# Another order of loads and side steps in an attention and two-MoE kernel: k and v over all partitions, rests of their own, a first h product in parts

## The chip, the cores and the metric

One core of one Trainium2 chip runs the kernel. The metric is device time of one execution in microseconds (us), lower is better. The engines are TensorE (PE, matmuls and transposes; PEld is its weight load), VectorE (DVE), ScalarE (ACT), GpSimd (POOL) and SyncE (SP, which here only issues DMAs). Each works through its own queue in order.

## What is computed

The reference in short:

```python
# q, k, v: [4, 8, 576, 64]
kv  = einsum('bhsd,bhse->bhde', k, v)
o   = einsum('bhsd,bhde->bhse', q, kv)
o   = o / sqrt(mean(o * o, -1) + 1e-6) * g_norm
x   = o.transpose(0, 2, 1, 3).reshape(2304, 512)
h   = x @ w_in                                  # [2304, 1024]
e   = exp(h - max(h));  so = h * e / (sum(e) + 1e-9)
ln  = (so - mean(so)) / sqrt(var(so) + 1e-6) * g_ln
x2  = ln @ w_out                                # [2304, 512]
out = ((x2 @ w_a) * (x2 @ w_b)) @ w_out2        # inner width 1536
```

The weights come as float64 and are made float32 on the chip.

## The kernel before

**Tiles.** The 2304 tokens are 18 tiles of 128. A batch has 576 tokens: four tiles of 128 and a rest of 64; the rests of two batches share a tile.

**Precision.** Most products are three matmuls: an operand is split into a high part (a copy by ACT into a shorter format, `split`, `x_hi`, `l_hi`) and a low part (source minus high, by DVE or POOL, lines 50, 423, 508, 552), and high x high, high x low, low x high are summed in PSUM.

**Weights.** `fetch` (line 272) loads a 128 x 512 block of float64 into one of five places of `ring`; a place is free again when the block that it held is narrowed. `begin` takes the absolute value on ACT (line 62), the class `Narrow` then clamps (line 67, DVE, or POOL where the order says BP), shifts (82), sets the sign (88) and adds the low bits (93) on DVE; `mid` does these steps for one block (M) or two side by side (MM), and `end` splits the block, its low part on POOL (E) or DVE (EV).

**Attention and first MoE.** These run by an order written out by hand, in the strings `PROLOGUE` (tiles 0 to 4), `SLOT` and `LATER` (one pass a tile). A token is a step: LK, LQ, LW load k and v, q, a weight block; kp multiplies a pair of heads of k and v and kk (DVE) or ka (ACT) keeps it; qt, qk turn q; op, os, om, ox are the o product, its squares, the root of the mean square (small steps on DVE, then ten on POOL) and the scaling (DVE); xt, xh, xl turn x and split it; hp is the h product (24 matmuls), hm, he, hs, hq, hn its maximum, exponential, product with it, squares and norm; lt0, lt1, lh0, ... turn and split the norm; yp, yk are the output product and its copy. "+2" is the tile two further on. An order string fixes the order on each engine's queue; between engines semaphores do.

**Loads of k and v.** `load_kv` loads half of the heads of a batch. The 576 rows of a head are laid over the partitions so that partitions 0 to 63 hold five rows and 64 to 127 hold four; so a tensor takes two DMAs, one for each half of the partitions (lines 317 and 318), and the fifth place of the upper half is zero, filled once (line 308). `kv_product` then does five chunks of two heads (line 342). Every third LK token does nothing.

**Second MoE.** It takes 6 tiles at once (s = 0, 1, 2) and two blocks of the inner width (j = 0 to 5). `quad(j, s, m, side)` is one product with w_a (m = 0) or w_b (m = 1), done as seven smaller products of six matmuls each, with additions by DVE between them (lines 740 to 765); the seventh is left open and closed in the quad that follows, after its third product. After each of the first six products `tick` runs some steps of the list `side` (weight narrowing, sums, splits for later quads), evenly dealt, and those that `then` put into `delayed` under t1 to t6, the tick's number. The last round prepares the output product, which `out_pair` does at the end (line 881).

Of the kernel before, what the change touches and what calls it, by code (L numbers as in the profile page):

```python
# [30 lines left out]
hp+2 qk+5 om+4 hq+1 E lh0 LW E xh+3 B MM lt1 LK ox+4 hn+1 hm+2 qt+6 ll0 he+2 lh1 qt+7 kp B xl+3 op+5  # L31
hs+2 kp hp+3 os+5 hq+2 om+5 ll1 hn+2 xt+4 LQ E qk+6 MM LK ka qk+7 B E kp lt0+1 lt1+1 ka xh+4 hm+3
ox+5 he+3 xl+4 op+6 lh1+1 ka lt1+2 lh0+1 B hs+3 ll0+1 os+6 lh1+2 E MM E ll1+1 lt0+2 xt+5 om+6 B EV
EV hp+4 BP hq+3 lh0+2 hm+4 he+4 ox+6 hn+3 hs+4 ll1+2 xh+5 yp yp yp yp xl+5 ll0+2 lt0+3 lt1+3 hq+4
lh0+3 yk yk hn+4 LK M yk E M ll0+3 B lh1+3 ll1+3 BP yk
"""
# [16 lines left out]
class Narrow:  # L53
# [47 lines left out]
def tile_attention_moe(ctx, tc, q, k, v, g_norm, w_in, w_out, g_ln, w_a, w_b, w_out2, out):  # L101
# [201 lines left out]
    KJ = -(-S // P)
    LONG = S - (KJ - 1) * P
    kv_tiles = [[ld.tile([P, H // 2, KJ, D], F32, name=f"{nm}s{n}", bufs=1) for nm in "kv"] for n in range(2)]
    for ts in kv_tiles:
        for t in ts:
            nc.gpsimd.memset(t[LONG:, :, KJ - 1, :], 0.0)
# [37 lines left out]

    def kv_keep(copy=nc.vector.tensor_copy):
# [42 lines left out]

    def o_rms(i):
# [4 lines left out]
        rms[i] = rsqrt(ms, H, "a")  # L396

# [33 lines left out]

    def h_product(i):
        xh, xl = xT.pop(i)
        ph = ps_h.tile([P, 2, HALF], F32, tag="h", name="ph")
        order = [(n, c) for n in range(2) for c in range(NK)]
        for n, c in order if i == 0 else sorted(order, key=lambda nc_: nc_[1]):
# [4 lines left out]
        hs_[i] = dict(ph=ph.rearrange("p a b -> p (a b)"))  # L441

# [546 lines left out]
    def load_gl(_):  # L989
# [178 lines left out]
    def half(n, part, eng=nc.vector):  # L1168
        return hi_lo(wo2, n, eng, part)
# [18 lines left out]
    for n, k in ((XB11, 0), (XT1, 1)):  # L1188
# [112 lines left out]
```

## Time and profile before

| | |
|---|---|
| time, median of 3 runs | 700.51 us (699.49 to 701.65) |
| profiled execution | 702.19 us, span 700.1 us |
| PE | 665.7 us busy, 95% of the span, 4710 instructions |
| PEld | 633.0 us, 90% |
| DVE | 519.6 us, 74% |
| ACT | 284.1 us, 41% |
| POOL | 302.8 us, 43% |
| mean granted PE clock | 0.995 of full speed |
| DMA | 103.84 MB, mean 148 GB/s |

The span is from the first to the last instruction of the profiled execution; the time has some 2 us more around it. Busy shares are means over stages with different limits: the start (loads and narrowing of w_in), the attention with the first MoE, the second MoE's rounds, and the output product. So the rows are read by stage.

### The profile page before, as it was taken

To read this page: it belongs to the slowest core of one execution; us is meant where nothing else is said; L and a number is where in the kernel's file an instruction comes from. 1 tells how busy PE (TensorE), PEld (TensorE's weight loads), DVE (VectorE), ACT (ScalarE), POOL (GpSimd) and SP (SyncE) were. 2 spreads that over 40 slices of the span, in tenths; PEclk is the share of its full clock that TensorE was granted. 3 is DMA by queue.
4 is the path that set the end of the run, shared out by engine and by line. 5 is a ranking of instruction groups with operands and counts; after the bars stand their busy time and mean duration, and the time that the engine had idled before them with its cause. 6 is when DMAs were issued, how large, how long until landed. Compare 5 with 4: busy or idle time off the path is not lost.

```text
span 700.1 us, 12578 instructions
## 1 busy us (share of the span) xinstructions
PE 665.7 (95%) x4710; PEld 633.0 (90%) x4710; DVE 519.6 (74%) x930; ACT 284.1 (41%) x491; POOL 302.8 (43%) x446
## 2 busy tenths in 40 slices
PE   1699999999999999999999999999999999999998
PEld 1577798999999998899999999999998899999998
DVE  3889977676688776779656867577656779987883
ACT  2558854544455346543331122212212445443431
POOL 2588776677666311113654467444672140000000
PEclk9899999999999999999999999999999999999999
DMA  9998645645542502342344336544334694654521
GB/s 248 316 248 234 184 127 156 168 127 149 178 127 76 167 16 68 106 136 81 111 149 136 118 106 187 177 136 142 112 95 129 221 313 139 190 146 130 150 76 61
DMA packets 107132, 103.84 MB, mean 148 GB/s; under 512 B 25280, under 2 KB 94400, under 8 KB 107072
## 3 DMA queue, kind: packets, MB, share of 16 engines
q1 hardware_dynamic: 101024, 94.40, 46.3%
q10 hardware_dynamic: 6048, 8.65, 3.7%
q8 instruction: 37, 0.61, 0.4%
q14 instruction: 23, 0.19, 0.1%
HBM read 71.05 MB, written 31.98 MB: 147 GB/s over the span
## 4 chain that ended last, share of the span: by engine, by line
PE 76%; DVE 9%; issue 5%; POOL 4%; DMA 3%; ACT 1%; SPq 1%; DVEq 0%; ACTq 0%; POOLq 0%
PE pw L710 26%; PE pq L881 18%; PE x2p L527 5%; PE x2p L525 5%; PE x2p L526 5%; PE ph L438 4%; PE ph L440 4%; PE ph L439 4%; PE ltp L495 2%; PE po L376 2%; DMA vs<-in_v_dram 1%; POOL a L751 1%; DMA wo<-w2d 1%; DMA gw<-gd 1%; PE xtp L413 1%
## 5 line engine op out<-in xcount | busy, mean ns | idle before, releaser
L751 POOL TENSOR_TENSOR a<-b,a 128x384 f32<-128x384 f32 x53 | 63.3, 1208 | 127.2 <-DVE b L740 126.2
L710 PE MATMUL pw<-xh,wh 128*128 128x384 f32 x336 | 114.3, 340 | 2.6 <-DVE b L761 1.6
L710 PE MATMUL pw<-xh,wl 128*128 128x384 f32 x336 | 112.7, 335 | 0.0
L710 PE MATMUL pw<-xl,wh 128*128 128x384 f32 x336 | 112.6, 335 | 0.0
L710 PE MATMUL pw<-x,wh 128*128 128x384 f32 x336 | 85.8, 336 | 0.9 <-DVE b L740 0.6
L525 PE MATMUL x2p<-lh,woh 128*128 128x256 f32 x288 | 82.6, 287 | 0.3 <-ACT lh L505 0.2
L526 PE MATMUL x2p<-ll,woh 128*128 128x256 f32 x288 | 80.6, 280 | 0.8 <-DVE ll L508 0.8
L527 PE MATMUL x2p<-lh,wol 128*128 128x256 f32 x288 | 80.6, 280 | 0.5 <-DVE wol L50 0.5
L710 PEld LDWEIGHTS pw<-xh,wh 128*128 128x128 f32 x336 | 63.1, 188 | 7.1 <-DVE b L761 2.3
L710 PEld LDWEIGHTS pw<-xl,wh 128*128 128x128 f32 x336 | 63.1, 188 | 0.0
L710 PEld LDWEIGHTS pw<-xh,wl 128*128 128x128 f32 x336 | 63.1, 188 | 0.0
L710 PEld LDWEIGHTS pw<-x,wh 128*128 128x128 f32 x336 | 60.5, 188 | 1.8 <-DVE b L740 0.9
L438 PE MATMUL ph<-wih,xh 128*128 128x512 f32 x144 | 56.9, 395 | 0.8 <-DVE so L461 0.8
L881 PE MATMUL pq<-wo,gh 128*128 128x256 f32 x336 | 57.7, 276 | 0.0
L440 PE MATMUL ph<-wih,xl 128*128 128x512 f32 x144 | 56.3, 391 | 1.2 <-DVE xl L423 1.2
L439 PE MATMUL ph<-wil,xh 128*128 128x512 f32 x144 | 56.3, 391 | 0.4 <-DVE wil L50 0.4
L710 PE MATMUL pw<-x,wl 128*128 128x384 f32 x168 | 56.2, 335 | 0.0
L527 PEld LDWEIGHTS x2p<-lh,wol 128*128 128x128 f32 x288 | 54.6, 190 | 0.9 <-DVE wol L50 0.9
L526 PEld LDWEIGHTS x2p<-ll,woh 128*128 128x128 f32 x288 | 54.2, 188 | 1.2 <-DVE ll L508 1.2
L525 PEld LDWEIGHTS x2p<-lh,woh 128*128 128x128 f32 x288 | 54.2, 188 | 0.9 <-ACT lh L505 0.5
L881 PE MATMUL pq<-wo,gw 128*128 128x256 f32 x450 | 53.1, 276 | 0.0
L67 POOL TENSOR_SCALAR nu<-nu 128x512 f32<-128x512 f32 x23 | 44.7, 1955 | 17.1 <-ACT nu L62 16.1
(158 smaller groups left out, 1536.0 us busy)
## 6 DMA issues: line engine op xcount, KB each, us to landing
gd<-a SPq DMA_DIRECT2D x72, 192.0 KB, 2.0
ring<-in_moe_w_out_dram SPq DMA_DIRECT2D x20, 512.0 KB, 5.4
gl<-gd SPq DMA_DIRECT2D x14, 384.0 KB, 3.5
gw<-gd SPq DMA_DIRECT2D x12, 384.0 KB, 3.2
ring<-in_moe_w_in_dram SPq DMA_DIRECT2D x8, 512.0 KB, 7.3
qs<-in_q_dram SPq DMA_DIRECT2D x16, 256.0 KB, 6.5
x2d<-x2s ACTq DMA_DIRECT2D x32, 128.0 KB, 1.8
st<-in_moe_w_a_dram SPq DMA_DIRECT2D x8, 512.0 KB, 4.3
```

The costliest lines, as they stand in the source:

```text
L67: eng.tensor_scalar(out=u, in0=u, scalar1=2.0 ** -15, scalar2=122879.9921875, op0=ALU.max, op1=ALU.min)
L376: nc.tensor.matmul(po[a:a + n, 2 * hp:2 * hp + 2, :], qT[i][:, hp, a:a + n], kvb[b % 3][:, hp, :], start=True, stop=True,)
L438: nc.tensor.matmul(ph[:, n, :], xh[:, c, :], wh, start=(c == 0), stop=False)
L439: nc.tensor.matmul(ph[:, n, :], xh[:, c, :], wl, start=False, stop=False)
L440: nc.tensor.matmul(ph[:, n, :], xl[:, c, :], wh, start=False, stop=(c == NK - 1))
L495: nc.tensor.transpose(pt[:, m, :], hs_[i]["so"][:, f * P:(f + 1) * P], ident)
L525: nc.tensor.matmul(pa, wh[:, cs], lh[:, f, :], start=(f == 0), stop=False)
L526: nc.tensor.matmul(pa, wh[:, cs], ll[:, f, :], start=False, stop=False)
L527: nc.tensor.matmul(pa, wl[:, cs], lh[:, f, :], start=False, stop=(f == NF1 - 1))
L710: nc.tensor.matmul(out, wt_[:, wn, c], xt_[xn][:, c], start=first and c == n == 0, stop=c == 1 and n == 2, skip_group_check=not first,)
L751: eng.tensor_tensor(out=a[n], in0=by, in1=a[n], op=ALU.mult)
L881: nc.tensor.matmul(ps, xt_[:, c], wt_[:, c], start=first and c == n == 0, stop=c == NJ - 1 and n == 2, skip_group_check=not first,)
```

## The change

1. `load_kv` now loads rows 0 to 511 of each head over all 128 partitions, four rows a partition, with one DMA a tensor into tiles of a pool with two buffers. The 64 rows that are left (the rests) of all eight heads are loaded by the new `load_rest`, 64 partitions, for k and v one DMA each, in the LK token that did nothing before. `kv_product` does four chunks and then the rest; the upper 64 partitions of the rest tiles are zero-filled once.
2. `PROLOGUE` is another order. The first h product is h0 to h7, one token for each block of w_in (three matmuls), with h6 ahead of h5. One clamp moves from POOL to DVE (wo0 and wo4 and e00 and e11 are POOL's now; wo0, wo1, wo3, e01 and e11 were), the low part of wo5 moves from POOL to DVE, one copy of a kv pair from DVE to ACT.
3. `quad` deals its side steps by the table `DEAL` where it has an entry for (s, m, number of steps): a digit a tick.
4. At the passage to the second MoE, hn of tile 16 comes before the first x split, hs of tile 17 before the weight split, hq after the first output product; hn and the transposes and splits of tile 17 become side steps of the first quad (ticks 1 and 5).
5. In the last round some steps move between ticks: two loads from t4 to t3 of one quad, the splits of WA11 and of WS1 one tick on, with splits of the last part of g pulled one tick ahead.
6. Minimum and maximum of the clamp change places; `o_rms` can take an engine (not used by the order).

The diff, cut:

```diff
 PROLOGUE = """
-LK LW B LW LQ BP M LK LK EV B MM qt kp qk LN LW kp kp LQ LW ka EV EV B ka LQ LQ kp kk M ka BP op os
-om B qt+1 E qk+1 LK LK B MM LQ E E ox op+1 qt+2 os+1 xt qk+2 LK LQ M xh qt+3 E B op+2 xl om+1 M qk+3
-os+2 om+2 EV ox+1 hp xt+1 BP xh+1 kp hm xl+1 op+3 kp qt+4 he os+3 BP ox+2 xt+2 hs ka hq xh+2 B om+3
-LQ LK LG LQ hn MM LK xl+2 hp+1 hm+1 ka qk+4 he+1 BP kp kp ox+3 kk kk qt+5 op+4 hs+1 lt0 xt+3 os+4
...
+LK LW B LW M LQ BP LK LK kp B MM EV LW qt kp LN qk LQ kp LW ka EV ka LQ EV B kk M LQ kp ka BP op LK
+os B om qt+1 M E B MM E qk+1 op+1 E os+1 ox qt+2 LQ qt+3 xt qk+2 LK xh E op+2 xl B om+1 M qk+3 os+2
+EV om+2 ox+1 LK h0 h1 LQ h2 h3 h4 h6 h5 h7 xt+1 BP xh+1 qt+4 kp hm kp xl+1 op+3 he os+3 B ox+2 hs hq
+LQ xt+2 LQ B LK LG xh+2 om+3 hn LK MM xl+2 ka hp+1 hm+1 B kp kp ox+3 ka qk+4 he+1 kk ka op+4 qt+5
...
+DEAL = {
+    (0, 0, 6): "121011",
+    (0, 1, 8): "312020",
+    (1, 0, 9): "231111",
+    (1, 1, 9): "122112",
+    (2, 0, 8): "221012",
+    (2, 1, 4): "111001",
+    (0, 0, 4): "102100",
+    (0, 1, 10): "113212",
+    (1, 0, 8): "321011",
+    (1, 1, 10): "033202",
+    (2, 0, 4): "111010",
+    (0, 0, 5): "003011",
+    (2, 0, 9): "233010",
+}
...
+    rest_tiles = [[ld.tile([P, H, D], F32, name=f"{nm}r{n}", bufs=1) for nm in "kv"] for n in range(2)]
...
     def load_kv(b, half):
...
+        ts = [ld.tile([P, H // 2, NS, D], F32, tag=nm, name=f"{nm}s") for nm in "kv"]
         for t, src in zip(ts, (k, v)):
-            of = src[b, h0:h0 + H // 2]
-            cut = LONG * KJ
-            nc.sync.dma_start(out=t[:LONG], in_=of[:, :cut, :].rearrange("h (p j) d -> p h j d", j=KJ))
             nc.sync.dma_start(
-                out=t[LONG:, :, :KJ - 1, :], in_=of[:, cut:, :].rearrange("h (p j) d -> p h j d", j=KJ - 1)
+                out=t, in_=src[b, h0:h0 + H // 2, :FULL, :].rearrange("h (p j) d -> p h j d", j=NS)
             )
         kvs[b, half] = ts
+
+    def load_rest(b):
...
+        for t, src in zip(ts, (k, v)):
+            nc.sync.dma_start(out=t[:REST], in_=src[b, :, FULL:S, :].rearrange("h s d -> s h d"))
+        rests[b] = ts
...
-            for j in range(KJ):
+            for j in range(NS):
...
+            for n in range(2):
+                h = 2 * hp + n
+                nc.tensor.matmul(pk[n * D:(n + 1) * D], kr[:, h, :], vr[:, h, :], start=False, stop=True)
...
-            for _ in range(-(-len(side) // ticks[0])):
+            for _ in range(-(-len(side) // ticks[0]) if deal is None else int(deal[6 - ticks[0]])):
                 side.pop(0)()
...
+    run("hn", i)
     all_of(side[:2])
-    run("hn", i)
     all_of(w_sums(0))
...
+    run("hs", i)
     all_of(w_split(0, nc.vector))
     all_of(side[10:])
-    run("hs", i)
+    run("yp yk hq", i)
     while pend:
         y_product(0)
         y_keep(0)
...
-    quad(0, 0, 0, [lambda: run("hq", i), lambda: None, lambda: run("hn", i)])
-    run("lt0 lt1 lh0 lh1 ll0 ll1", i)
+    none = [lambda: None]
+    quad(0, 0, 0, [lambda: run("hn", i), *3 * none, lambda: run("lt0 lt1 lh0 lh1 ll0 ll1", i), *none])
...
-        t1=[gl_(XB11, most), gl_(XT3, most)], t4=[gl_(XB22, most), gl_(XB21, most)], t6=early[:3],
+        t1=[gl_(XB11, most), gl_(XT3, most)], t3=[gl_(XB22, most), gl_(XB21, most)], t6=early[:3],
...
-        t2=half(WA11, 0), t3=[wl(WS2, w1, 2), *late_[:4]], t4=half(WA11, 1), t5=late_[4:8], t6=late_[8:],
+        t3=[wl(WS2, w1, 2), *half(WA11, 0), *late_[:4]], t4=[*half(WA11, 1), *late_[4:8]], t6=late_[8:],
...
-        t1=half(WS1, 0), t2=half(WS1, 1), t3=[second_place], t4=[wl(WA12, w2, 0, nc.scalar), *half(WS2, 0)],
+        t2=half(WS1, 0), t3=[second_place, *half(WS1, 1)], t4=[wl(WA12, w2, 0, nc.scalar), *half(WS2, 0)],
```

## Rows read from the trace of the kernel before

**Rows 1.** Stage windows: length, busy us (instructions) of PE, PEld, DVE, ACT, POOL, clock, DMA, GB/s.
```profile
12.00:29.00 17.00, 9.21 (x108) 7.86 (x107) 14.20 (x28) 10.19 (x22) 8.19 (x13) 0.90 1.09 305
29.00:41.00 12.00, 9.83 (x40) 7.63 (x40) 10.99 (x18) 4.17 (x8) 8.84 (x16) 0.86 1.11 275
41.00:87.00 46.00, 42.53 (x350) 35.57 (x351) 42.85 (x86) 35.38 (x67) 36.43 (x73) 1.00 0.80 216
...
260.00:300.00 40.00, 37.90 (x279) 35.84 (x278) 28.92 (x54) 23.77 (x39) 6.18 (x10) 1.00 0.24 77
...
500.00:560.00 60.00, 57.49 (x322) 55.15 (x321) 42.68 (x76) 16.77 (x30) 22.35 (x19) 1.00 0.43 133
```

**Rows 2.** Chain that ended last, its start: start us, us, what.
```profile
9.07 9.10 DMA vs<-in_v_dram
```

**Rows 3.** DMA packets in 13.5 to 16.5 (k, v), 24 to 24.5 (q), 363 to 365.5 (w_b).
```profile
DMA packets 657, 0.70 MB, mean 234 GB/s; under 512 B 35, under 2 KB 657, under 8 KB 657
...
DMA packets 576, 0.14 MB, mean 287 GB/s; under 512 B 576, under 2 KB 576, under 8 KB 576
...
DMA packets 1014, 0.92 MB, mean 369 GB/s; under 512 B 29, under 2 KB 1014, under 8 KB 1014
```

**Rows 4.** Timeline of PE at the start: start us, us, line, what [idle before, releaser].
```profile
18.30 1.77 PE L342 MATMUL kvp<-vs,ks 128*64 128x64 f32 x40 [3.13 <-DMA vs<-in_v_dram]
...
29.21 1.04 PE L413 MATMUL xtp<-ident,x 128*128 128x128 f32 x4 [3.25 <-DVE x L403]
...
30.89 1.92 PE L376 MATMUL po<-kvb,qT 128*128 128x128 f32 x8
...
34.50 0.50 PE L440 MATMUL ph<-wih,xl 128*128 128x512 f32 x1 [1.20 <-DVE xl L423]
...
39.96 0.50 PE L439 MATMUL ph<-wil,xh 128*128 128x512 f32 x1 [0.45 <-DVE wil L50]
```

**Rows 5.** Timeline of DVE at the start.
```profile
10.28 0.43 DVE L67 TENSOR_SCALAR nu<-nu 128x512 f32<-128x512 f32 x1 [10.28 <-ACT nu L62]
...
13.60 0.69 DVE L50 TENSOR_TENSOR wil<-nu,wih 128x512 fp32r<-128x512 f32 x1 [0.69 <-ACT wih L49]
...
15.22 1.28 DVE L88 SCALAR_TENSOR_TENSOR nu<-ring,nu 128x512 uint32<-128x512 uint32 x2
...
28.46 0.69 DVE L403 TENSOR_TENSOR x<-po,y_a 128x512 f32<-128x512 f32 x1 [0.94 <-POOL y_a L203]
...
38.22 0.68 DVE L393 TENSOR_REDUCE ss<-sq 128x8 f32<-128x512 f32 x1
```

**Rows 6.** Timeline of ACT at the start.
```profile
30.29 0.69 ACT L418 ACTIVATE xh<-xtp,gn 128x512 fp32r<-128x512 f32 x1 [1.14 <-PE xtp L413]
...
38.34 0.62 ACT L49 CAST wih<-nu 128x512 fp32r<-128x512 f32 x1 [2.35 <-DVE nu L93]
```

**Rows 7.** PE's waits from 240 to 500: for whom, us in total, times, longest.
```profile
PE ltp L495 <- ACT so L486: 1.5, 2, 0.9
PE pw L710 <- DVE b L761: 0.4, 1, 0.4
PE x2p L526 <- DVE ll L508: 0.3, 1, 0.3
```

**Rows 8.** Timeline of DVE at the passage to the second MoE.
```profile
266.81 1.00 DVE L552 TENSOR_TENSOR xl<-xf,xh 128x768 fp32r<-128x768 f32 x1 [3.14 <-ACT xh L587]
...
278.88 2.10 DVE L552 TENSOR_TENSOR wl<-w0s,wh 128x1024 fp32r<-128x1024 f32 x2
```

**Rows 9.** PE's waits from 500 to the end.
```profile
PE pw L710 <- DVE b L761: 1.3, 1, 1.3
PE pw L710 <- DVE b L740: 0.6, 1, 0.6
PE pw L710 <- DVE b L765: 0.3, 1, 0.3
```

**Rows 10.** Timeline of DVE in the last round.
```profile
548.25 0.96 DVE L552 TENSOR_TENSOR wo<-wo 128x768 fp32r<-128x768 f32 x1 [2.31 <-ACT wo L869]
```

More of the change, by code (lines that the diff above doesn't have):

```diff
@@ L26 @@
 PROLOGUE = """
[L27 to L35 removed]
+LK LW B LW M LQ BP LK LK kp B MM EV LW qt kp LN qk LQ kp LW ka EV ka LQ EV B kk M LQ kp ka BP op LK
+os B om qt+1 M E B MM E qk+1 op+1 E os+1 ox qt+2 LQ qt+3 xt qk+2 LK xh E op+2 xl B om+1 M qk+3 os+2
+EV om+2 ox+1 LK h0 h1 LQ h2 h3 h4 h6 h5 h7 xt+1 BP xh+1 qt+4 kp hm kp xl+1 op+3 he os+3 B ox+2 hs hq
+LQ xt+2 LQ B LK LG xh+2 om+3 hn LK MM xl+2 ka hp+1 hm+1 B kp kp ox+3 ka qk+4 he+1 kk ka op+4 qt+5
+hs+1 lt0 xt+3 os+4 qk+5 lh0 om+4 hp+2 E hq+1 E MM ll0 qt+7 lt1 ox+4 hn+1 hm+2 xh+3 LW BP LK lh1 qt+6
+he+2 kp xl+3 op+5 hs+2 B kp os+5 hq+2 om+5 hp+3 qk+6 MM hn+2 LK B LQ xt+4 E ka qk+7 kp ka lt0+1 E
+lt1+1 xh+4 hm+3 xl+4 he+3 op+6 lh1+1 ox+5 ll1 lh0+1 B hs+3 ll0+1 lt1+2 ka MM os+6 ll1+1 E EV lh1+2
+lt0+2 hp+4 BP xt+5 om+6 B EV EV hq+3 lh0+2 hm+4 he+4 ox+6 hn+3 xh+5 yp yp yp xl+5 hs+4 yp ll1+2
+ll0+2 hq+4 lt0+3 hn+4 LK B yk lt1+3 lh0+3 yk M yk M ll0+3 lh1+3 ll1+3 BP E yk
 """
@@ L67, in clamp @@
         eng.tensor_scalar(
-            out=u, in0=u, scalar1=2.0 ** -15, scalar2=122879.9921875, op0=ALU.max, op1=ALU.min
+            out=u, in0=u, scalar1=122879.9921875, scalar2=2.0 ** -15, op0=ALU.min, op1=ALU.max
         )
@@ L185, in tile_attention_moe @@
     kvb = [wt.tile([P, NP, P], F32, name=f"kvb{n}") for n in range(3)]
-    for t in kvb:
+    rest_tiles = [[ld.tile([P, H, D], F32, name=f"{nm}r{n}", bufs=1) for nm in "kv"] for n in range(2)]
+    for t in [*kvb, *(t[REST:] for ts in rest_tiles for t in ts)]:
         nc.gpsimd.memset(t, 0.0)
@@ L299, in tile_attention_moe @@
     kvs = {}
+    rests = {}
     qs = {}
     qT = {}
[L303 to L308, printed above, removed]
     def load_kv(b, half):
         h0 = half * (H // 2)
-        ts = kv_tiles[half]
+        assert b == 0 or all((b - 1, hp) in multiplied for hp in range(half * NP // 2, (half + 1) * NP // 2))
+        ts = [ld.tile([P, H // 2, NS, D], F32, tag=nm, name=f"{nm}s") for nm in "kv"]
         for t, src in zip(ts, (k, v)):
-            of = src[b, h0:h0 + H // 2]
-            cut = LONG * KJ
-            nc.sync.dma_start(out=t[:LONG], in_=of[:, :cut, :].rearrange("h (p j) d -> p h j d", j=KJ))
             nc.sync.dma_start(
-                out=t[LONG:, :, :KJ - 1, :], in_=of[:, cut:, :].rearrange("h (p j) d -> p h j d", j=KJ - 1)
+                out=t, in_=src[b, h0:h0 + H // 2, :FULL, :].rearrange("h (p j) d -> p h j d", j=NS)
             )
         kvs[b, half] = ts
+    def load_rest(b):
+        assert b < 2 or all((b - 2, hp) in multiplied for hp in range(NP))
+        ts = rest_tiles[b % 2]
+        for t, src in zip(ts, (k, v)):
+            nc.sync.dma_start(out=t[:REST], in_=src[b, :, FULL:S, :].rearrange("h s d -> s h d"))
+        rests[b] = ts
     def load_q(i):
@@ L337, in kv_product @@
             kt, vt = kvs[b, hp // 2]
+            kr, vr = rests[b]
             pk = ps_t.tile([P, NP, P], F32, tag="t", name="kvp")[:, 0, :D]
-            for j in range(KJ):
+            for j in range(NS):
                 for n in range(2):
@@ L342, in kv_product @@
                     nc.tensor.matmul(
-                        pk[n * D:(n + 1) * D], kt[:, h, j, :], vt[:, h, j, :], start=(j == 0), stop=(j == KJ - 1)
+                        pk[n * D:(n + 1) * D], kt[:, h, j, :], vt[:, h, j, :], start=(j == 0), stop=False
                     )
+            for n in range(2):
+                h = 2 * hp + n
+                nc.tensor.matmul(pk[n * D:(n + 1) * D], kr[:, h, :], vr[:, h, :], start=False, stop=True)
             kvps.append((b, hp, pk))
+            multiplied.add((b, hp))
     def kv_keep(copy=nc.vector.tensor_copy):
@@ L353, in kv_keep @@
             ready.add((b, hp))
-    ready = set()
+    ready, multiplied = set(), set()
     psum_of = {}
@@ L389, in tile_attention_moe, with o_rms @@
     rms = {}
-    def o_rms(i):
+    def o_rms(i, eng=nc.gpsimd):
         ss = sm.tile([P, H], F32, name="ss")
@@ L395, in o_rms @@
         nc.vector.tensor_scalar(out=ms, in0=ss, scalar1=1.0 / D, scalar2=1e-6, op0=ALU.mult, op1=ALU.add)
-        rms[i] = rsqrt(ms, H, "a")
+        rms[i] = rsqrt(ms, H, "a", eng)
     xt = {}
@@ L430, in tile_attention_moe, with h_product @@
     hs_ = {}
-    def h_product(i):
-        xh, xl = xT.pop(i)
-        ph = ps_h.tile([P, 2, HALF], F32, tag="h", name="ph")
+    def h_product(i, part=slice(None)):
+        if i not in hs_:
+            hs_[i] = dict(ps=ps_h.tile([P, 2, HALF], F32, tag="h", name="ph"))
+            hs_[i]["ph"] = hs_[i]["ps"].rearrange("p a b -> p (a b)")
+        ph = hs_[i]["ps"]
+        xh, xl = xT[i]
         order = [(n, c) for n in range(2) for c in range(NK)]
-        for n, c in order if i == 0 else sorted(order, key=lambda nc_: nc_[1]):
+        order = order if i == 0 else sorted(order, key=lambda nc_: nc_[1])
+        for n, c in order[part]:
             wh, wl = wi[n, c]
@@ L440, in h_product @@
             nc.tensor.matmul(ph[:, n, :], xl[:, c, :], wh, start=False, stop=(c == NK - 1))
-        hs_[i] = dict(ph=ph.rearrange("p a b -> p (a b)"))
     def h_max(i):
@@ L729, in quad @@
         ticks = [6]
+        deal = DEAL.get((s, m, len(side)))
         def tick():
-            for _ in range(-(-len(side) // ticks[0])):
+            for _ in range(-(-len(side) // ticks[0]) if deal is None else int(deal[6 - ticks[0]])):
                 side.pop(0)()
@@ L971, in tile_attention_moe @@
     for b in range(B):
-        kv_loads += [(load_kv, b, 0), None, (load_kv, b, 1)]
+        kv_loads += [(load_kv, b, 0), (load_rest, b), (load_kv, b, 1)]
     q_loads = list(range(NTILE))
@@ L976, in next_kv @@
         if kv_loads:
-            fn = kv_loads.pop(0)
-            if fn:
-                fn[0](*fn[1:])
+            fn, *args = kv_loads.pop(0)
+            fn(*args)
     def next_q(_):
@@ L997, in tile_attention_moe @@
         kp=kv_product, kk=lambda _: kv_keep(), ka=lambda _: kv_keep(nc.scalar.copy),
-        qt=q_turn, qk=q_keep, op=o_product, os=o_square, om=o_rms, ox=o_scale, xt=x_turn, xh=x_hi, xl=x_lo,
-        hp=h_product, hm=h_max, he=h_exp, hs=h_solu, hq=h_square, hn=h_norm,
+        qt=q_turn, qk=q_keep, op=o_product, os=o_square, om=o_rms, omd=lambda i: o_rms(i, nc.vector), ox=o_scale, xt=x_turn, xh=x_hi, xl=x_lo,
+        hp=h_product, **{f"h{n}": lambda i, n=n: h_product(i, slice(n, n + 1)) for n in range(8)}, hm=h_max, he=h_exp, hs=h_solu, hq=h_square, hn=h_norm,
         lt0=lambda i: l_turn(i, 0), lt1=lambda i: l_turn(i, 1),
```

## The prediction

> **What bounds the kernel now.** I read the stage windows first, then the chain of work that ended last, then the waits of each engine. TensorE (PE) is busy for most of the span, so the first question is where it is not: the reader subtracts PE's busy time from the length of each window of [rows 1]. PE lacks 7.8 us between 12 and 29 us, 2.2 us between 29 and 41 (at a mean granted clock of 0.86, so some of its work there ran at the lower level), 3.5 us between 41 and 87, 2.1 us between 260 and 300 and 2.5 us between 500 and 560. Elsewhere it is nearly full. A change can therefore gain in four places: the loads at the start, VectorE's (DVE's) narrowing of w_in behind them, the passage from the first to the second MoE, and the last round of the second MoE.
>
> At the start the chain is a load: the second half of v of batch 0 is 9.1 us on its way [rows 2] and PE waits 3.1 us for it, at 18.30 [rows 4]. After that the chain runs over DVE. It begins at 10.28, when the first w_in block is there [rows 5], and ends when the low part of w_in's last block lets PE go on at 39.96 [rows 4]. In 41 to 87 DVE is busy 42.9 of 46 us, as much as PE [rows 1]: there both are close to being the bound.
>
> **The loads.** A half of k and v is 2 x 4 heads x 576 x 64 floats, 1.18 MB. Now each of its four DMAs writes 64 partitions, with rows of 1280 or 1024 bytes, and moves at 234 GB/s, the first row of [rows 3]: 5.0 us a half. After the change a half is two DMAs over 128 partitions with 1024-byte rows, 1.05 MB. The nearest row is w_b in the second MoE, 1024-byte rows into 128 partitions: 369 GB/s, the third of [rows 3], so 2.8 us, a gain of 2.2 us a half. If the row length, not the partitions, set the rate, it stays 234 GB/s and 4.5 us, a gain of 0.5. I take 369, because that row has the same row length and only the partitions differ.
>
> The rests are new: 0.26 MB a batch, 256-byte rows into 64 partitions. q's 256-byte rows into 128 partitions go at 287 GB/s, the second of [rows 3]: 0.9 us if only row length matters; at half of that, as 64 partitions suggest, 1.8 us. I take 1.4. Before the second half of v lies now 2.2 + 2.2 - 1.4 = 3.0 us less (between 3.5 less and 0.8 more); before the first w_in block 2.2 us less.
>
> The trace shows that 64 partitions go with 234 GB/s and 128 with 369, but the two transfers differ in more than that. [...]
>
> PE does the same ten matmuls a head pair (five chunks of two heads before, four and a rest after), so nothing there. The zero fills on GpSimd (POOL) grow from 64 x 256 to 64 x 512 but end before POOL has other work: nothing. SP issues six DMAs a batch instead of eight: nothing, as a load is on its way for far longer than its issue takes.
>
> **The first h product.** PE's order hardly changes (h6 before h5, some transposes swapped, all single matmuls kept), so running it in parts costs nothing. What changes is DVE's order before it. Step by step, for the time at which w_in's last low part is done: DVE starts 2.2 us earlier. Its wait of 0.69 for the high part of block 0 is filled, since that low part now follows the next pair of blocks, and its wait of 0.94 for the root of tile 0 is filled by a whole pair of blocks (clamp 0.43, shift about the same, twice 1.28 a pair: 4.3 us) put ahead [rows 5]: 1.6. The sums of tile 2 (0.68 and two small ones, 1.0) go behind it. Against this, the low part of x of tile 0 now comes right behind the scaling, so DVE waits for the transposes (1.04) and the high part (0.69) [rows 4, 6]: 1.7 lost; and the last low part has nothing between it and its high part any more, 0.62 [rows 6]. Sum: 2.2 + 1.6 + 1.0 - 1.7 - 0.6 = 2.5 us. PE does not stand against it: it waited until 34.50 for the low part of x, which now comes right behind the scaling, and before the first part of the h product stands only the third o product (1.92) [rows 4].
>
> From 41 to 87 DVE gets one more clamp (0.43) and one more low part (0.69), and gives two copies to ScalarE (ACT); POOL has one clamp and one low part less. What is queued behind these DVE steps is the low part and sums on which PE's first output products wait. I book 0 there, between 0.6 lost and 1.0 gained, since both engines are near full. **Front: 2.5 us, between 0.5 and 3.8.**
>
> **The passage to the second MoE.** PE waits 1.5 us in two places for the normalized tile from ACT and 0.3 for the low part behind it [rows 7]. At 266.81 DVE is busy with an x split that waited 3.1 us for ACT, and the norm's small steps stand behind it [rows 8]; the change puts the norm first. For the last tile it puts the softmax product ahead of the weight split (2.10 [rows 8]) and norm and transposes into the first quad, between its products. The cover is six products of six matmuls at 0.18 (57.49 us over 322 matmuls in [rows 1]), 1.07 us each: the norm has four of them, the copies one. The weight split ends about 1.6 us later, still before the quad starts. Without cover, what is lost is one of the two waits, 0.9. **1.8 us, between 0.9 and 2.1.**
>
> **The last round.** PE waits 1.3, 0.6 and 0.3 us for additions that stand behind splits on DVE [rows 9]. At 548.25 a w_out split, after 2.3 us of waiting for ACT and its load, stands ahead of such an addition [rows 10]; the change moves these splits one tick down, behind it, and empties the fifth tick. That is the 0.6 and the 0.3. The load moved from the fourth tick to the third passes no other DMA on SP, since in that quad none is issued between, so the 1.3 stays. **0.8 us, between 0 and 0.9.**
>
> **The rounds.** The dealt side steps end one wait of 0.4 [rows 7], where a clamp stood before an addition: the copies that it needs now start a tick later, behind the addition. Steps that are dealt three to a tick can make new ones. **0.3 us, between 1 lost and 0.5 gained.** Swapping minimum and maximum costs nothing.
>
> Sum: 2.5 + 1.8 + 0.8 + 0.3 = 5.4 us. The profiled execution took 702.19 (span 700.1, 2.1 around it) and would take 696.8; the median of the runs is 700.51, 1.7 less than the profiled one, and becomes 695.1.
>
> **Rivals.** (a) The front's gain is given back: DVE is busy 93% between 41 and 87, and its added steps and displaced waits eat the 2.5. Left are 2.9: 697.6. For it speaks DVE's share; against it that all of DVE's work moves forward with the loads and POOL is relieved. (b) The second MoE's waits only move: another step is late in their place. Left are 2.5: 698.0. For it: in-order queues; against: slack of several products. (c) The loads do not get faster: rate set by rows, rests on top. Then DVE starts 0.5 earlier, not 2.2, and the front gives 0.8: 696.8. (d) Slower: the new deal puts up to three DVE steps before an addition in each of the 24 quads of four full rounds. One such wait costs 0.4 [rows 7]; in every quad that is 9.6, so 695.1 + 9.6 = 704.7. It decides from 14 such waits (5.4 / 0.4). Against it: with up to two steps a tick the list of waits shows one of them in all rounds.
>
> **How the numbers follow.** Forecast 0.58, (a) 0.17, (b) 0.10, (c) 0.09, (d) 0.06. The range takes (a), (b), (c) and the bounds of the terms in: 691.2 (all terms at their best, 3.8 + 2.1 + 0.9 + 0.5 = 7.3, and 2 us for waits that also vanish) to 698.6. A measurement can tell 0.3%, 2.1 us, from no change: faster means below 698.4. Forecast and (c) are nearly all below, (a) and (b) mostly: 0.85; same 0.10; slower 0.05.
>
> **What would show it.** Right, step by step: packets of the k and v loads near 370 GB/s; DVE's first clamp near 8 us and PE's wait at 18.30 gone or near 15.5; the last w_in part near 37.5; no wait for the normalized tile near 265 to 290; no waits for additions but the one of 1.3 near 530. Wrong: k and v still near 240 GB/s; PE's idle time between 41 and 87 (3.5 now) grown by the front's gain; new waits for additions in each round. The prediction fails most easily at the front, where three in-order queues were reordered at once.

## The result and the profile after

The changed kernel takes 688.62 us, median of 4 runs (687.39 to 689.73), against 700.35 us (699.49 to 701.65, 4 runs) before: a ratio of 0.9831, 95% interval 0.9808 to 0.9853, 11.7 us less. In a second measurement (experiment 12) it was 0.9809 (0.9788 to 0.9829). The forecast was 695.1 us with a low end of 691.2: the direction was right, and the gain is more than twice the 5.4 us forecast. The profiled execution has a span of 686.5 us, 13.6 us less than that of before; the latter took 702.19 us, 1.8 over the median of its kernel, so the pair of traces shows some 2 us more than the medians do. TensorE (PE) does the same 4710 instructions. One execution, of the three front edits together (experiment 11), ran slow, with 1110.81 us at a mean granted clock of 0.562, and enters no ratio and no reading below.

The stage windows of after, to be laid beside [rows 1] (length, then busy us and instructions of PE, PEld, DVE, ACT, POOL, clock, DMA share, GB/s):

```profile
12.00:29.00 17.00, 11.29 (x99) 10.19 (x100) 14.92 (x30) 9.30 (x20) 6.73 (x13) 0.80 1.04 332
29.00:41.00 12.00, 10.59 (x89) 7.99 (x87) 9.62 (x17) 5.75 (x10) 9.86 (x24) 1.00 1.03 325
41.00:87.00 46.00, 42.47 (x326) 35.85 (x325) 41.79 (x86) 36.59 (x71) 29.80 (x72) 1.00 0.67 198
260.00:300.00 40.00, 40.00 (x299) 38.91 (x298) 28.98 (x50) 24.99 (x40) 8.98 (x10) 1.00 0.29 92
500.00:560.00 60.00, 59.20 (x356) 58.56 (x355) 44.71 (x73) 21.60 (x36) 24.77 (x19) 1.00 0.62 198
```

By the matmul column, from 29 to 41 PE is busy for 10.59 us, before 9.83, and with 89 matmuls instead of 40, at a granted clock of 1.00 instead of 0.86; the passage at 260 to 300 is full; the last round lacks 0.8 us of PE instead of 2.5.

DMA packets of after in 3 to 5 us (k, v) and 10 to 12.2 us (nearly all 256-byte rows: q and the rests together), which answer to [rows 3]:

```profile
DMA packets 764, 0.77 MB, mean 383 GB/s; under 512 B 16, under 2 KB 764, under 8 KB 764
...
DMA packets 2126, 0.61 MB, mean 277 GB/s; under 512 B 2032, under 2 KB 2124, under 8 KB 2126
```

Timeline of DVE at the start of after, beside [rows 5] (start, duration, line, what, in brackets the idle time before and its releaser):

```profile
8.25 0.43 DVE L82 TENSOR_SCALAR nu<-nu 128x512 f32<-128x512 f32 x1 [8.25 <-ACT nu L77]
...
30.11 0.75 DVE L443 SCALAR_TENSOR_TENSOR xl<-xtp,gn,xh 128x512 fp32r<-128x512 f32 x1 [1.73 <-ACT xh L438]
...
35.72 0.69 DVE L65 TENSOR_TENSOR wil<-nu,wih 128x512 fp32r<-128x512 f32 x1 [0.69 <-ACT wih L64]
```

and of PE, beside [rows 4]:

```profile
12.96 0.48 PE L363 MATMUL kvp<-vr,kr 128*64 128x64 f32 x4 [5.80 <-DMA vr<-in_v_dram]
...
36.46 0.50 PE L463 MATMUL ph<-wil,xh 128*128 128x512 f32 x1 [0.23 <-DVE wil L65]
...
83.27 0.39 PE L550 MATMUL x2p<-lh,wol 128*128 128x256 f32 x1 [0.81 <-DVE wol L65]
```

DVE's first clamp is at 8.25 instead of 10.28; no pair of heads waits for the second half of v any more (the wait of 3.1 at 18.30 is gone), though the first pair now waits for the rest; the last low part of w_in lets PE go on at 36.46 instead of 39.96.

**Where the rest came from** is not in these rows. It is in the waits of the weight loads (PEld), which I had not read. Before, from 240 us to the end (for whom, us in total, times, longest):

```profile
PEld pw L710 <- DVE b L740: 2.8, 5, 0.9
PEld pw L710 <- DVE b L761: 2.6, 3, 1.6
PEld ltp L495 <- ACT so L486: 2.3, 2, 1.2
PEld pw L710 <- DVE b L765: 1.3, 4, 0.6
PEld pw L710 <- DVE a L765: 1.1, 3, 0.5
PEld x2p L526 <- DVE ll L508: 0.5, 1, 0.5
PEld pw L710 <- DVE a L761: 0.5, 1, 0.5
PEld x2p L525 <- ACT lh L505: 0.5, 1, 0.5
PEld ltp L495 <- issue: 0.2, 1, 0.2
PEld po L376 <- issue: 0.2, 1, 0.2
```

and after, from 235 us to the end, all there is:

```profile
PEld pw L733 <- DVE b L785: 0.8, 1, 0.8
PEld pw L733 <- DVE a L764: 0.6, 1, 0.6
PEld ltp L518 <- issue: 0.2, 1, 0.2
PEld po L396 <- issue: 0.2, 1, 0.2
```

These lists add up to 12.0 and 1.8 us. The difference of 10.2, with the 3.5 us that PE is ahead at 36.46, is 13.7 us; the spans differ by 13.6. For the same waits PE's matmul row lists 1.5, 0.4 and 0.3 [rows 7] and 1.3, 0.6 and 0.3 [rows 9], 4.4 us; with three more of 0.2 each, which those rows leave out, it is 5.0. The window from 300 to 500 us of before, and below it that of after, show the same (columns as above): the matmul row lacked 1.0 us of 200 before, the weight-load row 4.1.

```profile
300.00:500.00 200.00, 199.03 (x1146) 195.91 (x1146) 139.49 (x239) 53.68 (x88) 102.63 (x90) 1.00 0.45 138
```
```profile
300.00:500.00 200.00, 200.00 (x1154) 199.84 (x1153) 146.97 (x256) 51.19 (x85) 109.43 (x94) 1.00 0.45 137
```

How a wait hides in the matmul row is seen in one place of before, PE's timeline in the second MoE:

```profile
368.29 0.34 PE L710 MATMUL pw<-xh,wh 128*128 128x384 f32 x1
368.46 0.34 PE L710 MATMUL pw<-xl,wh 128*128 128x384 f32 x1
368.64 0.34 PE L710 MATMUL pw<-xh,wl 128*128 128x384 f32 x1
369.35 0.45 PE L710 MATMUL pw<-xh,wh 128*128 128x384 f32 x1 [0.37 <-DVE b L761]
```

Matmuls begin every 0.175 us, but each record is 0.34 long, so records overlap. Between 368.64 and 369.35 lie 0.71 us where 0.175 is normal: 0.54 lost at this place, of which the row calls 0.37 idle. PEld lists 0.7 for it. Shorter waits, of 0.5 us and less in PEld's list, are 0.2 or 0.3 in that of the matmul row or don't appear there: from 240 to 500 it has one wait of 0.2 for the additions of L740 and none for those of L765.

### The profile page after: what moved, and what is told of

Read it like the earlier page. It is cut to its first block, busy times and chain, and to the rows that moved or that the text cites. A ratio compares the mean times of both kernels' runs of the same rounds, so it can differ in the third digit from the quotient of the medians.

```text
span 686.5 us, 12566 instructions
## 1 busy us (share of the span) xinstructions
PE 660.6 (96%) x4710; PEld 634.1 (92%) x4710; DVE 519.4 (76%) x930; ACT 283.5 (41%) x493; POOL 274.6 (40%) x444
## 4 chain that ended last, share of the span: by engine, by line
PE 87%; DVE 5%; DMA 3%; issue 1%; ACT 1%; POOL 1%; SPq 1%; DVEq 0%; ACTq 0%; POOLq 0%
PE pw L733 37%; PE pq L905 19%; PE x2p L550 5%; PE x2p L548 5%; PE x2p L549 5%; PE ph L462 4%; PE ph L463 4%; PE ph L464 4%; DMA ring<-in_moe_w_in_dram 2%; PE ltp L518 2%; PE po L396 2%; PE qtp L382 1%; DMA qs<-in_q_dram 1%; PE xtp L433 1%; DVE nu L103 1%
## 5 line engine op out<-in xcount | busy, mean ns | idle before, releaser
L733 PE MATMUL pw<-xh,wh 128*128 128x384 f32 x336 | 112.9, 336 | 0.8 <-DVE b L785 0.5
L548 PEld LDWEIGHTS x2p<-lh,woh 128*128 128x128 f32 x288 | 54.2, 188 | 0.3 <-ACT xh L438 0.2
L549 PEld LDWEIGHTS x2p<-ll,woh 128*128 128x128 f32 x288 | 54.2, 188 | 0.0
L905 PEld LDWEIGHTS pq<-wo,gw 128*128 128x128 f32 x450 | 52.0, 188 | 0.0
```

What stands on the lines that cost most here:

```text
L548: nc.tensor.matmul(pa, wh[:, cs], lh[:, f, :], start=(f == 0), stop=False)
L549: nc.tensor.matmul(pa, wh[:, cs], ll[:, f, :], start=False, stop=False)
L733: nc.tensor.matmul(out, wt_[:, wn, c], xt_[xn][:, c], start=first and c == n == 0, stop=c == 1 and n == 2, skip_group_check=not first,)
L905: nc.tensor.matmul(ps, xt_[:, c], wt_[:, c], start=first and c == n == 0, stop=c == NJ - 1 and n == 2, skip_group_check=not first,)
```

## The experiments

Ratios are to the kernel before on the same chip (701.5 to 702.2 us, medians of 7 to 21 runs), with 95% intervals.

**Theories.** A: the front, the passage and the rounds are three places, and each part removes PE's idle time of its own; the rounds' idle time is what PEld shows. B: all gain comes through the front (a start moved ahead), and the rounds move with it. C: the parts share one gain; for it speaks that the parts alone gain 16.9 us by their ratios, and the whole 11.8 to 13.4.

**1. The loads alone** (`load_kv`, `load_rest`, `kv_product`, zero fills, and the LK tokens' work):

```diff
-                out=t[LONG:, :, :KJ - 1, :], in_=of[:, cut:, :].rearrange("h (p j) d -> p h j d", j=KJ - 1)
...
+                out=t, in_=src[b, h0:h0 + H // 2, :FULL, :].rearrange("h (p j) d -> p h j d", j=NS)
```

> Only the loads of k and v and the rests are changed, all else is as before. Theory (the front's gain is DVE starting earlier): k and v move near 380 GB/s, DVE's first clamp comes at 8.3 us instead of 10.3, and the low part of w_in's last block 1.5 to 2.5 us earlier; time 1.5 to 2.5 us under before. Rival (the order of the steps is what gives the front's gain, DVE being the bound there): the loads land earlier, the last low part does not, time within 0.7 us of before.

Measured: 0.9966 (0.9952 to 0.9980), 2.4 us less. DVE's first clamp is at 7.93 and its last low part of w_in at 36.99 (39.22 before), so the loads do what they should; PE goes on behind that low part at 38.71, in a stretch (29 to 41) with a mean granted clock of 0.71.

**2. The order of the prologue alone**, with the old loads:

```diff
...
-os+2 om+2 EV ox+1 hp xt+1 BP xh+1 kp hm xl+1 op+3 kp qt+4 he os+3 BP ox+2 xt+2 hs ka hq xh+2 B om+3
+EV om+2 ox+1 LK h0 h1 LQ h2 h3 h4 h6 h5 h7 xt+1 BP xh+1 qt+4 kp hm kp xl+1 op+3 he os+3 B ox+2 hs hq
...
```

> Only the order of the prologue (with the first h product in parts) is changed, loads and clamp as before. Theory (loads and order add up): filled waits of DVE give 1.0 to 1.5 us. Rival (the order is what gives the gain): 3 us or more. Second rival (the order needs the earlier loads): slower than before by up to 1 us, as DVE waits for blocks that are not there yet.

Measured: 0.9985 (0.9970 to 1.0000), 1.1 us, hardly told from none. The last low part of w_in is waited for until 38.95 (39.96 before).

**3. The clamp alone**, and **4. the kernel after with the old clamp**:

```diff
-            out=u, in0=u, scalar1=2.0 ** -15, scalar2=122879.9921875, op0=ALU.max, op1=ALU.min
+            out=u, in0=u, scalar1=122879.9921875, scalar2=2.0 ** -15, op0=ALU.min, op1=ALU.max
```

> Only minimum and maximum of the clamp change places. Theory booked before the result: nothing. Rival, from the trace of after, where a clamp on POOL takes 0.61 us instead of 1.93: POOL's clamps fall to 0.61 here too; where POOL holds up the start (second block, fifth block) the low part of w_in's last block comes up to 1.5 us earlier, and the time falls by 0.5 to 2 us. If POOL had slack everywhere, its busy time falls by some 30 us and the time stays within 0.7 us.

> The changed kernel with minimum and maximum as before. If the clamp carries part of the gain: 1 to 3 us over the changed kernel, 690 to 692 us. If it only empties POOL: within 0.7 us of the changed kernel, near 688.6 us.

Measured: 0.9993 (0.9980 to 1.0007) and 0.9824 (0.9808 to 0.9841; after has 0.9831 and 0.9809). Nothing that a measurement tells in either, yet POOL's clamp itself got three times shorter. The groups of POOL's clamps in before, in the clamp alone and in after with the old clamp (how many, busy us, mean ns, idle time before):

```profile
L67 POOL TENSOR_SCALAR nu<-nu 128x512 f32<-128x512 f32 x23 | 44.7, 1955 | 17.1 <-ACT nu L62 16.1
```
```profile
L67 POOL TENSOR_SCALAR nu<-nu 128x512 f32<-128x512 f32 x23 | 14.6, 648 | 21.0 <-ACT nu L62 20.1
```
```profile
L82 POOL TENSOR_SCALAR nu<-nu 128x512 f32<-128x512 f32 x22 | 43.5, 1990 | 13.6 <-ACT nu L77 12.6
```

It follows the order of the two operations, which is all that these edits change. 30 us of POOL's time are saved and the kernel is not faster by what can be told: POOL had slack there.

**5. Is it the partitions or the rows that set the loads' rate?** After, with each k and v load cut into two of 64 partitions; the rows keep their 1024 bytes:

```diff
+            rows = src[b, h0:h0 + H // 2, :FULL, :].rearrange("h (p j) d -> p h j d", j=NS)
+            for p in (slice(0, P // 2), slice(P // 2, P)):
+                nc.sync.dma_start(out=t[p], in_=rows[p])
```

> The changed kernel with each k and v load as two DMAs of 64 partitions, rows of 1024 bytes all the same. Theory (the partitions set the rate): k and v fall back to 235 to 250 GB/s and the first clamp comes near 10 us, time 1 to 2.5 us over the changed kernel. Rival (the uneven rows of 1280 and 1024 bytes set the rate; in the changed kernel the rests move at 288 GB/s into 64 partitions, which speaks for it): k and v stay near 380 GB/s and the time is that of the changed kernel within 0.7 us.

Measured: 0.9853 (0.9830 to 0.9876); packets in 3 to 5 and in 15.5 to 16.5:

```profile
DMA packets 573, 0.55 MB, mean 277 GB/s; under 512 B 32, under 2 KB 573, under 8 KB 573
...
DMA packets 250, 0.24 MB, mean 240 GB/s; under 512 B 16, under 2 KB 250, under 8 KB 250
```

DVE's first clamp is back at 10.58. So it is not the length of the rows: 1024 bytes went at 383 GB/s into 128 partitions and at 240 to 277 into 64. The size of a DMA falls with the partitions here (512 to 256 KB) and was not varied by itself. The faster rate is worth 1.5 us by the ratio to the first measurement of after, which the intervals don't tell from none, and 3.1 by that to the second.

**6. The deal alone** (the table and its use in `tick`), and **7. the kernel after without it**:

```diff
...
+            for _ in range(-(-len(side) // ticks[0]) if deal is None else int(deal[6 - ticks[0]])):
```

> Only the side steps of the quads are dealt by the table; all else as before. Booked in the prediction: 0.3 us. Theory now (stalls that TensorE's matmul row hides, since records of matmuls overlap, while its weight loads stand idle): the rounds give 3 to 5 us, weight loads busy 99% and more between 300 and 500 us instead of 98%, matmuls' idle time there smaller by 1 us only. Rival (the rounds' gain comes from POOL being relieved or from earlier loads upstream): within 1 us of before.

> The kernel after with the side steps dealt evenly again (no DEAL table), all else kept. Theory 1, the deal removes idle time of PE's weight loads that every round has of its own (PEld busy 195.9 of 200 us between 300 and 500 before, 199.8 after): the time grows by 4 to 7 us over the kernel after, ratio to before 0.989 to 0.993, and PEld between 300 and 500 falls back to 196 to 197. Rival, the parts share one gain (their single gains add up to some 17 us, the whole change gives 11.8): leaving one out costs less than 3 us, ratio below 0.9875.

Measured: 0.9901 (0.9877 to 0.9925) alone, 6.9 us and more than the 3 to 5 expected, and without it 0.9873 (0.9848 to 0.9898), that is 3 to 4.5 us more than after by the medians of the ratios; this is less than the 4 to 7 expected, and by its ratio it falls just on the rival's side. The windows from 300 to 500 of the deal alone, of after without the deal, and of deal and passage together (experiment 12):

```profile
300.00:500.00 200.00, 199.58 (x1161) 198.92 (x1160) 141.83 (x244) 53.61 (x88) 105.87 (x90) 1.00 0.46 137
```
```profile
300.00:500.00 200.00, 198.25 (x1126) 194.32 (x1125) 141.96 (x247) 51.18 (x83) 104.20 (x90) 1.00 0.45 136
```
```profile
300.00:500.00 200.00, 200.00 (x1157) 199.79 (x1157) 144.33 (x250) 52.93 (x87) 106.01 (x90) 1.00 0.45 137
```

PEld is at 198.9 or more in the nine traces with the table, and between 193.8 and 195.9 in the eight without it. This part of theory A is shown: the table, and not the earlier start, removes the rounds' waits.

**8. The passage alone**, and **9. the kernel after with the old passage**:

```diff
...
-    quad(0, 0, 0, [lambda: run("hq", i), lambda: None, lambda: run("hn", i)])
-    run("lt0 lt1 lh0 lh1 ll0 ll1", i)
+    quad(0, 0, 0, [lambda: run("hn", i), *3 * none, lambda: run("lt0 lt1 lh0 lh1 ll0 ll1", i), *none])
```

> Only the passage from the first to the second MoE is changed. Booked: 1.8 us. Theory (the weight loads' wait counts, 2.3 us for ACT's tile and 1.0 for the splits behind it): 3 to 3.7 us. Rival (the booked idle time of the matmul row is right): 1.5 to 2.1 us.

> The kernel after with the old passage to the second MoE, all else kept. Alone the passage gave a ratio of 0.9925 (some 5 us), in the traces 2.3 us at the first quad of the second MoE. Theory 1, the passage is a place of its own: leaving it out costs 2 to 3.5 us, ratio 0.986 to 0.988, and the loss lies before the second quad. Theory 2, the shift of the rounds that it brings is worth something beyond its place: 5 us, ratio near 0.990, with part of the loss later than the second quad. Rival, nothing: the time of the kernel after.

Measured: 0.9925 (0.9900 to 0.9950) alone, 5.3 us and more than the 3 to 3.7 expected; after with the old passage 0.9847 (0.9827 to 0.9868). In the trace of the latter the waits of PEld at the passage are all back:

```profile
PEld ltp L518 <- ACT so L509: 2.3, 2, 1.2
...
PEld x2p L549 <- DVE ll L531: 0.5, 1, 0.5
PEld x2p L548 <- ACT lh L528: 0.5, 1, 0.5
```

3.3 us, and with the new passage none of them is left. By the ratios the old passage costs 1.1 to 2.7 us, in part less than the 2 to 3.5 expected.

**10. The last round alone**:

```diff
...
-        t1=half(WS1, 0), t2=half(WS1, 1), t3=[second_place], t4=[wl(WA12, w2, 0, nc.scalar), *half(WS2, 0)],
+        t2=half(WS1, 0), t3=[second_place, *half(WS1, 1)], t4=[wl(WA12, w2, 0, nc.scalar), *half(WS2, 0)],
```

> Only the last round's steps are moved. Booked: 0.8 us, the wait of 1.3 near 533 stays. Theory (weight loads): 1.5 to 3 us. Rival: the changed rounds ahead of it, not the moved steps, took the waits away, and this kernel gains under 1 us.

Measured: 0.9990 (0.9972 to 1.0008), 0.7 us, not told from none: the rival stands, not the 1.5 to 3 us.

**11. The three front edits together** (loads, order and clamp), measured twice:

> The loads, the order of the prologue and the clamp together, nothing of the second MoE's edits. Alone the three measured ratios of 0.9966, 0.9985 and 0.9993 to the kernel before, some 4 us in all. If the order only works on the earlier blocks (DVE starts 2.2 us earlier and every later DVE step follows), they add up: ratio 0.993 to 0.996, the last low part of w_in done near 36.5 us instead of 39.96, and PE 3.5 us ahead at 83 us. If the loads' gain and the order's are the same wait taken twice, the three give no more than the loads alone: ratio 0.9965 or above and the low part near 38 us.

> Loads, order and clamp together, for a trace. If their gain lies in the front alone, the first quad of the second MoE comes 4 to 5 us earlier and the end 4 to 5 us, ratio 0.993 to 0.994, and the 0.9899 was a chance of few runs. If the ratio is 0.990 again, 2 to 3 us must show between the first quad and the end: fewer waits of the weight loads for additions between 300 and 560 us (11 us before between 240 and 700), without any edit there.

Measured: 0.9899 (0.9876 to 0.9922) and 0.9928 (0.9905 to 0.9951). The last low part of w_in is waited for until 36.30, as in after. On DVE loads and order add up there: that low part begins at 39.22 before, 2.2 us earlier with the loads, 1.0 with the order, 3.7 with all three edits. The first quad comes 4.3 us earlier than before, the end 5.5. From 300 to 500 the edits gain nothing: PEld is at 194.54, less than before's 195.91. Why so is seen in its waits from 345 to 375, of PEld, DVE and ACT:

```profile
PEld pw L718 <- DVE b L769: 1.2, 1, 1.2
PEld pw L718 <- DVE b L748: 1.0, 2, 0.5
...
DVE st L67 <- ACT st L62: 6.7, 3, 3.6
...
ACT st L62 <- DMA st<-in_moe_w_a_dram: 1.8, 1, 1.8
```

ACT waits for a load of w_a, DVE's clamp of it waits for ACT, and the addition that PE needs stands behind the clamp. Before's own profile has 0.7 of ACT's wait there. The table puts such clamps behind the additions.

**12. Deal and passage together, and the whole beside its halves:**

> The deal and the passage, nothing else. Alone they gave ratios of 0.9901 and 0.9925. If these are places of their own, together 0.982 to 0.984 (11 to 12 us). If both remove the same idle time of the rounds, 0.987 to 0.990 (7 to 9 us).

> The kernel after, unchanged, on the chip on which its two halves run. The halves' theories are told by their sums: if front and second MoE are places of their own, the gain is the sum of the two halves' gains (7 us of the front's three edits, 6 to 9 of the deal and the passage): ratio 0.977 to 0.981. If they share one gain, the ratio stays at 0.983 as measured first.

Measured: 0.9863 (0.9843 to 0.9883), 9.6 us, and 0.9809 for the whole, 13.4 us. The ratios alone don't settle it: 0.9863 lies between the two ranges expected, 0.9809 at the edge of the one for places of their own. The front's three edits gave 5.1 us on that chip, and 7.1 at the first measurement there: with 9.6 and 0.7 (last round) that is 15.4 or 17.4, against 13.4 and intervals of 1.3 to 1.6 us on each. Deal and passage gave 6.9 and 5.3 alone and 9.6 together, a gap of 2.6 us.

**The traces settle it, place by place.** The start of the same matmul can be read in PE's timeline of every run; four marks cut the second half into three stretches. In before they are the last matmul of o (po) at 246.06, the first matmul behind the last output product at 304.06, the 1261st of the 1512 matmuls of pw at 520.48, with which the last round begins, and the last of these at 572.05. What follows takes 128.0 us in every trace. Lengths in us over the 17 traces:

| stretch | before | after | all without its edit | all with its edit |
|---|---|---|---|---|
| passage | 57.99 | 54.58 | 57.1 to 58.0 (8 traces) | 54.2 to 54.6 (9) |
| rounds (the table) | 216.43 | 212.50 | 216.4 to 218.4 (8) | 212.5 to 213.3 (9) |
| last round | 51.57 | 49.01 | 48.5 to 51.6 (8) | 48.2 to 49.9 (9) |

With the 3.68 us by which that matmul of o comes earlier in after, the pair of before and after differs by 3.7 + 3.4 + 3.9 + 2.6 = 13.6 us. Passage and rounds each follow their own edit, whatever the other edits are, and the weight-load row had both right (3.3 and 3.9). So theory A holds for these, and theories B and C have fallen there. The last round doesn't follow its edit: before's 51.57 is the longest of all, and the other kernels without edit and table have 49.1 to 50.2. If before often has this stretch so long, every part that shifts it would gain these 1.4 to 2.5 us, and the sum of the parts would count them several times; that would explain the gaps above, but before was traced once, and this is not shown.

PEld's waits of deal and passage from 500 on are the two that follow, without the edit of the last round:

```profile
PEld pw L725 <- DVE a L777: 0.5, 1, 0.5
PEld pw L725 <- DVE a L781: 0.3, 1, 0.3
```

**13. Two more steps moved behind one that PE waits for**, after otherwise:

```diff
...
-lt0+2 hp+4 BP xt+5 om+6 B EV EV hq+3 lh0+2 hm+4 he+4 ox+6 hn+3 xh+5 yp yp yp xl+5 hs+4 yp ll1+2
+lt0+2 hp+4 BP xt+5 B EV EV om+6 hq+3 lh0+2 hm+4 he+4 ox+6 hn+3 xh+5 yp yp yp xl+5 hs+4 yp ll1+2
...
-    then(t1=early[3:4], t2=early[4:6], t3=early[6:7], t4=early[7:8], t5=early[8:10])
+    then(t2=early[3:6], t3=early[6:7], t4=early[7:8], t5=early[8:10])
```

> The kernel after with two more steps moved behind a step that PE waits for: the sums for tile 6's mean square behind the last two low parts of w_out in the prologue (PE waited 0.8 us for these at 83 us), and one subtraction of the last round from the first tick to the second (PE waited 0.5 us for the addition behind it). If the waits go, 0.5 to 1.3 us less than the kernel after, ratio 0.981 to 0.9825; if the moved steps are late in their new place, the same time or up to 1 us more.

> The kernel after with the two moved steps, beside the kernel after on one chip. If the moved steps gain, 0.5 to 1.3 us less than after_again; if not, within 0.5 us of it, since the first trace of it shows the weight load's wait of 0.9 us for the addition still in its place.

Measured: 0.9804 (0.9781 to 0.9828) and, beside after's 688.06 us, 688.55 us. No gain. PE's waits from 60 to 90 say why for the first step:

```profile
PE x2p L548 <- DVE va L501: 1.5, 1, 1.5
...
PE x2p L550 <- DVE wol L65: 0.2, 1, 0.2
```

The wait of 0.8 for the low part of w_out fell to 0.2, and one of 1.5 for the norm of another tile stands beside it. The weight loads' wait of 0.9 for the addition in the last round stands in the first trace as before, and in the second it is gone; it is gone too in three kernels that don't have this edit (experiments 4, 5 and 9), so it comes and goes without it.

## Why the prediction was right and wrong, point by point

**Loads: right.** 383 GB/s measured, 369 taken, 234 the other end; experiment 5 shows that it isn't the rows and leaves partitions and size of a DMA. No slowing of the rests is seen: 256-byte rows run at 277 GB/s, close to q's 287 [rows 3], not at half of it; but rests and q move together in that stretch. k and v cut in halves ran at 240 to 277 GB/s into 64 partitions, against 383 into 128, while these rests, moved beside q, show no such drop: no run shows the half of q's rate behind the 1.8 us, the slower of the two values between which I took 1.4. DVE began 2.03 us earlier; the sum said 2.2.

**The first h product: near by size, in part by luck.** 3.5 us instead of 2.5, inside the 0.5 to 3.8. Two terms of the sum can be read off: 1.7 lost while DVE waits for the high part of x was 1.73, and the 0.6 lost ahead of the last low part was 0.69. Of the 1.6 for waits that would be filled, less than 1 came: 0.69, 0.40, 0.44 and 0.94 stood there before, and 0.68, 0.73 and 0.40 stand in after beside the two that were booked. Between the first clamp and the last low part DVE is idle for 4.8 us, before for 3.3. What became shorter is its work there, from 25.69 to 22.65 us: the sums of tile 2 are 1.0 of that, as booked, and the other 2.0 had no term. They are steps that run longer before. Three that follow one another take 3.9 us, where the same steps take 0.43, 0.43 and 0.69 at 20.00, 10.74 and 20.93:

```profile
29.07 0.88 DVE L67 TENSOR_SCALAR nu<-nu 128x512 f32<-128x512 f32 x1
29.99 1.38 DVE L82 TENSOR_SCALAR nu<-nu 128x512 uint32<-128x512 uint32 x1
31.41 1.66 DVE L88 SCALAR_TENSOR_TENSOR nu<-ring,nu 128x512 uint32<-128x512 uint32 x1
```

POOL makes low parts at that time; in after DVE stands waiting for x while POOL makes them. Whether POOL is the cause was not tried.

PE's granted clock had no term in my sum: its mean fell from 0.90 to 0.80 in 12 to 29 and rose from 0.86 to 1.00 in 29 to 41. In before's windows of 1 us from 12 to 41 it is 0.50 (20 to 22 and 30 to 32) or 1.00 of full speed, but for the four in which it changes. Rival (a) didn't come in this trace: the lead of 3.5 us at 36.46 is still there at 83.27, where before waited until 86.72 for the same matmul. But in the six traces with these loads and this order the lead at that matmul is 1.6 to 4.0 us. The two with 3.5 and 4.0 have a mean granted clock of 1.00 and 0.98 in 29 to 41, the four with 1.6 to 2.6, the second trace of after (2.2) among them, 0.89 or 0.90. So what is left of the front's gain goes with the clock of the execution, which was not varied by itself. Rival (c) is excluded by the 383 GB/s.

**The passage: right in mechanism, mis-sized.** I booked 1.8 us, with an upper end of 2.1, from waits of 1.5 and 0.3 in the matmul row [rows 7]. PEld lists 2.3, 0.5 and 0.5 for the same places, 3.3 us, and all of it went. The passage alone gained 5.3 us by its ratio (1.75 either way), and taking it out of after cost 1.1 to 2.7 by the medians of the ratios; 3.3 lies between, and the stretch became 3.4 shorter (experiment 12).

**The rounds: the step that failed.** I read "nearly full" from the matmul windows and one wait of 0.4 [rows 7], and booked 0.3. PEld has 4.1 us of idle time in 300 to 500 alone, 3.6 of it in nine waits for additions of 0.2 to 0.7, where the matmul row lists two, of 0.4 and 0.2; after has 0.2 us of idle time there. By the starts of the matmuls the rounds became 3.9 us shorter, 3.1 to 5.9 between any trace without the table and any with it; by ratios it is worth 3 to 7 us, the most of any single edit. Rival (d) had the mechanism, an in-order queue with steps ahead of an addition, with the wrong sign: the even deal was the one that made such waits.

**The last round: mis-sized in before, small by itself.** Of the 4.6 us of PEld's waits before between 500 and 560 after has 1.4. But the edit alone gives 0.7 us, and deal and passage without it have 0.8 us of these waits left. Most of what the pair of traces shows here is thus not the edit's. "The 1.3 stays" was wrong: PE's wait at that place (533.36 in before) is gone in after, whose 0.5 stands at another (551.33). Nor is it the edit that ended it: the other kernels without the edit lose at most 0.5 us there. In before the subtraction ahead of that addition had waited 1.17 us for a load of g (DMA gw<-gd, at 532.01), in after 0.15.

**The clamp: right for the time**, 0.5 us that a measurement can't tell; wrong if "costs nothing" is read as "changes nothing" (1955 to 626 ns on POOL, in after).

Put together with the right row: 2.5 (front) + 3.3 (passage) + 3.9 (rounds) + some 0.7 (last round, the measured value, not told from none) = 10.4 us against 11.7 measured. Of the 6.3 us that the forecast of 5.4 lacked, 5 came from one choice, the row from which PE's idle time was read, and 1.0 from the front. Rival (b) didn't come either: of the second MoE's waits none moved into the rounds, and 1.4 us by the weight loads stand in the last one. The top of the range, 698.6, did not follow from the terms: their low ends, 0.5 + 0.9 + 0 - 1.0, leave 0.4 us and 700.1.

## What to carry to other kernels

Read the room that PE has left from the weight-load row and its waits, or from the starts of matmuls, never from busy matmul time: here 1.0 us of idle time in the one row was 4.1 in the other, and the rounds became 3.9 us shorter. In a loop whose matmuls each wait for an addition on an in-order engine, put the side steps that may wait themselves (a clamp behind a load) after the addition, by hand and for each length of the list; dealing evenly looked harmless and cost more than the loads did (the table alone gave 6.9 us, the loads alone 2.4). A load that fills half of the partitions, as k and v did here at 234 GB/s, should be laid over all of them (383 here), with the remainder as a small load of its own.

## What the runs showed of the hardware that was not expected

POOL's two-operation clamp of 128x512 floats takes 1.96 to 1.99 us with max first and min second, and 0.63 to 0.65 us with min first; DVE's takes the same either way (655 and 651 ns for the clamps of st). Why was not tried. DMAs into 64 partitions with rows of 1024 bytes ran at 240 to 277 GB/s and into 128 at 383.
